# One level of Strassen's algorithm for the second product of a fused attention and ELU kernel

## The chip, the cores and the metric

The kernel runs on one core of one Trainium2 chip. The metric is device time in microseconds (us). Five engines are named as the profile names them: PE (TensorE matmuls; PEld is its weight loads), DVE (VectorE), ACT (ScalarE), POOL (GpSimd) and SP (SyncE, which issues most DMAs).

## The reference

```python
# x: (8, 8, 512, 64) float32, state: (8, 8, 32, 64) float32      B, H, S, D and 32 states
scores = x @ state.T / 8;   a  = softmax(scores);   xread = a @ state     # per batch and head
scores2 = state @ x.T / 8;  a2 = softmax(scores2);  sread = a2 @ x
t = concat([xread, sread], axis=2)         # (8, 8, 544, 64), as a matrix (8*544, 512)
h = t @ w_in                               # w_in (512, 2048)
g = where(h > 0, h, exp(min(h, 0)) - 1)    # ELU
out = g @ w_out                            # w_out (2048, 512)
```

Output: 4352 rows of 512 float32. The weights arrive as float64, and the kernel makes float32 of them.

## The kernel before, in words

Each of the 8 batches has 512 tokens. For a batch the kernel computes both softmaxes (`attention`), folds `state` into `w_in` (`make_m`, tile `m_sb`), and then runs two products. The **first product** (`ffn1`) makes 16 tiles h of 128 hidden features by 512 tokens, with two matmuls each, in a PSUM pool of three banks. ACT and DVE make the ELU of each tile (`exp_part`: two ACT passes into `e_sb`; `max_part`: one DVE pass into `g_sb`). The **second product** (`ffn2_part`) takes the 16 tiles of `g_sb` as weights in four chunks of 128 tokens; each chunk accumulates 16 matmuls of 512 columns of `w_out` in one PSUM bank, and `ffn2_end` copies the bank to `o_sb`. The 8*32 state rows go last (`states`): a first product with 256 columns and two chunks of the second product.

Batch 0 (`first_batch`) follows a plan written out by hand, beside which ACT and DVE convert the weights; its second product runs all four chunks together. From batch 1 on, PE and SP keep the order in which the program is written, while a scheduler orders ACT, DVE and POOL. Inside the second product of batch b the steps of the attention of batch b+1 are hung in as hooks, one after every four matmuls of the code: two steps of transposes of x (`xT_ps`), the scores (`s_ps`, followed by the softmax on DVE, ACT and POOL), two empty ones, the transposes of the state softmax (`sT_ps`), the state read (`sr_ps`), the load of x for batch b+2; `full_m` (`m_ps`) is hung in at chunk 3. They share one PSUM slot of two banks, `ps_a`. Batch 7 has no hooks.

A matmul of the code in float32 is two MATMUL records in the trace, each with its own LDWEIGHTS, so a batch's second product is 4*16*2 = 128 records. Nearly all instructions are recorded through one helper, and so have one line, L93; they are told apart by their tiles.

Of the kernel before, what the change touches and what calls it, by code (L numbers as in the profile page):

```python
# [10 lines left out]
FP32 = mybir.dt.float32  # L11
# [4 lines left out]
ALU = mybir.AluOpType  # L16
# [9 lines left out]
def kernel(  # L26
# [31 lines left out]
    out_b = out.rearrange("(b s) c -> b s c", b=B)  # L58
# [4 lines left out]
    def pool(name, bufs, **kw):  # L63
        return ctx.enter_context(tc.tile_pool(name=name, bufs=bufs, **kw))

    cpool = pool("const", 1)
    xpool = pool("x", 2)
    apool = pool("attn", 2)
    atspool = pool("aT_s", 1)
    xtpool = pool("xT", 2)  # L70
    atpool = pool("aT", 4)
    mpool = pool("m", 2)
    rawpool = pool("raw", NRAW)
    small = pool("small", 4)
    gpool = pool("g", FO + 1)
    epool = pool("elu", 4)
    opool = pool("o", 2)
    ps_a = pool("ps_a", 1, space=PSUM)
    ps_h = pool("ps_h", 3, space=PSUM)
# [30 lines left out]
    w_in = cpool.tile([P, NP, DF], FP32, name="w_in")  # L110
    w_out = cpool.tile([P, FO, DM], FP32, name="w_out")

    kT = cpool.tile([P, B, P], FP32, name="kT")

    xT_state = cpool.tile([P, NP, B * NS], FP32, name="xT_state")
# [9 lines left out]
            )  # L125

    def load_states():
        raw = rawpool.tile([P, B, G, D], FP32, tag="raw", name="s_sb")
        s_v = state.rearrange("b (m c) n d -> m c n b d", c=G)
        for m in range(NP):  # L130
            for c in range(G):
                sync.dma_start(out=raw[m * NS : (m + 1) * NS, :, c], in_=s_v[m, c])
        return raw
# [5 lines left out]

    def load_weights(src):  # L140
        k = src.shape[-1]
        raw = rawpool.tile([P, 512], moe_w_in.dtype, tag="raw", name="raw")
        sync.dma_start(out=raw.rearrange("p (j k) -> p j k", k=k), in_=src)
        return raw

# [54 lines left out]
        st[b, "xT", i] = ps  # L200

    def copy_x(b, i):
        xT = xtpool.tile([P, 2, R * P], FP32, name="xT")
        for j in range(2):
            st[b, 2 * i + j] = xT[:, j]
            scalar.copy(
                out=xT[:, j], in_=st[b, "xT", i][:, j].rearrange("p r q -> p (r q)")
            )
# [84 lines left out]
                transpose(ps[:, g, r], a[:, r])  # L293

    def copy_state(b):
        st[b, "aT_s"] = atspool.tile([P, G, R, P], FP32, name="aT_s")
        for g in range(G):
            scalar.copy(out=st[b, "aT_s"][:, g], in_=st[b, "sT"][:, g])

# [30 lines left out]
    def full_m(b, c):  # L330
        make_m(b, c)
        copy_m(b, c, (scalar.copy, vector.tensor_copy))

    def elu(ps, g, fo):

        e = exp_part(ps)
        max_part(g, fo, e, ps)

    def exp_part(ps):
        e = epool.tile([P, ps.shape[-1]], FP32, tag="e", name="e_sb")  # L340
        scalar.activation(out=e, in_=ps, func=AF.Relu, scale=-1.0)
        scalar.activation(out=e, in_=e, func=AF.Exp, scale=-1.0)
        return e

    def max_part(g, fo, e, ps):
        g[fo] = gpool.tile([P, ps.shape[-1]], FP32, tag="g", name="g_sb")
        vector.scalar_tensor_tensor(
            out=g[fo], in0=e, scalar=-1.0, in1=ps, op0=ALU.add, op1=ALU.max
        )

    def ffn1(g, b, fo):

        ps = ps_h.tile([P, S], FP32, tag="h", name="h_ps")
        for k in range(G):
            matmul(
                ps,
                m_t[b, fo // 4][:, k, fo % 4 * P : (fo % 4 + 1) * P],
                st[b, k, "aT"],
                start=(k == 0),
                stop=(k == G - 1),  # L360
            )
        return ps

    def ffn1_state(g, fo):

# [9 lines left out]
        elu(ps, g, fo)

    def ffn2_part(g, chunks, ps, fos, hooks=(), every=1):

        done = 0
        for fo in fos:  # L380
            for c in chunks:
                matmul(
                    ps[c],
                    g[fo][:, c * P : (c + 1) * P],
                    w_out[:, fo],
                    start=(fo == 0),
                    stop=(fo == FO - 1),
                )
                done += 1
                if hooks and done % every == 0:  # L390
                    hooks.pop(0)()

    def o_bank():
        return ps_o.tile([P, DM], FP32, tag="o", name="o_ps")

    def ffn2_end(chunks, ps, o_sb):
        for c in chunks:
            (scalar.copy, vector.tensor_copy)[c % 2](out=o_sb[c // 2][:, c % 2], in_=ps[c])

    def attention(b):  # L400

# [19 lines left out]

    def store(b, i, o_sb):
        rows = out_b[b, 0:S].rearrange("(p r) c -> p r c", r=R)
        sync.dma_start(out=rows[:, 2 * i : 2 * i + 2], in_=o_sb[i])

    def two_o():
        return [opool.tile([P, 2, DM], FP32, name="o_sb") for i in range(2)]

    def first_batch():

# [24 lines left out]
        for c in range(1, FC + 1):  # L455
            if c < FC:
                order += [lambda c=c, n=n: load_w_in(c, n) for n in range(NP)]
            order += [lambda fo=fo: load_w_out(fo) for fo in range(4 * c - 4, 4 * c)]
        w, h, e, g = [], {}, {}, {}

        def fetch():
            if len(w) == 28:
# [18 lines left out]
        for step in plan:  # L481
            name, _, num = step.partition(":")
            num = [int(i) for i in num.split(".") if i]
            if name == "kT":
                turn_states(raw_states)
            elif name == "kTc":
                vector.tensor_copy(out=kT, in_=st["k_ps"])
                fetch()
            elif name in groups:
                groups[name](*num)  # L490
            elif name in whole:
                whole[name](*num)
            elif name == "w":
                (convert_1, convert_2)[num[1] - 1](*w[num[0]])
                if num[1] == 2:
                    fetch()
            elif name == "F":
                h[num[0]] = ffn1(g, 0, num[0])
            elif name == "R":
                e[num[0]] = exp_part(h[num[0]])  # L500
            elif name == "E":
                max_part(g, num[0], e[num[0]], h[num[0]])
            elif name == "O":
                ffn2_part(g, range(R), o_ps, num)
            elif name == "x":
                turn_x(*num)
            elif name == "M":
                make_m(*num)
            elif name == "xc":
                copy_x(*num)  # L510
            else:
                assert name == "Mc", step
                copy_m(*num, (scalar.copy, scalar.copy))
        copy_m(1, 0, (scalar.copy, vector.tensor_copy))
        o_sb = two_o()
        ffn2_end(range(R), o_ps, o_sb)
        for i in range(2):
            store(0, i, o_sb)

    def batch(b):  # L520
        g = {}
        for fo in range(FO):
            elu(ffn1(g, b, fo), g, fo)
# [6 lines left out]
        o_sb = two_o()  # L530
        for c in range(R):
            if nxt and c == R - 1:
                hooks += [lambda: full_m(b + 1, 0)]
            ps = {c: o_bank()}
            ffn2_part(g, [c], ps, range(FO), hooks, 4)
            ffn2_end([c], ps, o_sb)
            if c % 2:
                store(b, c // 2, o_sb)
        for f in hooks:
            f()  # L540

    def states():
        g = {}
        for fo in range(FO):
            ffn1_state(g, fo)
        o_sb = [opool.tile([P, 2, DM], FP32, name="o_sb")]
        for c in range(2):
            ps = {c: o_bank()}
            ffn2_part(g, [c], ps, range(FO))
            ffn2_end([c], ps, o_sb)  # L550
            for i in range(P // NS):
                sync.dma_start(
                    out=out_b[c * (P // NS) + i, S:SB], in_=o_sb[0][i * NS : (i + 1) * NS, c]
                )
# [38 lines left out]
```

## Time and profile before

| | |
|---|---|
| median of 3 runs | 862.76 us (862.56 to 862.92) |
| the profiled execution's own time | 862.39 us |
| its span | 860.6 us |
| PE busy | 823.3 us, 96% |
| DVE, ACT, POOL busy | 275.8, 303.1, 35.5 us (32%, 35%, 4%) |
| mean granted TensorE clock | 0.994 of 2.4 GHz |

The span is the recorded part of the execution; 1.8 us lie around it. Busy shares say how much an engine does, and the chain of waits says on which engine the end hung.

### The profile page before, as it was taken

To read this page: it belongs to the slowest core of one execution; us is meant where nothing else is said; L and a number is where in the kernel's file an instruction comes from. 1 tells how busy PE (TensorE), PEld (TensorE's weight loads), DVE (VectorE), ACT (ScalarE), POOL (GpSimd) and SP (SyncE) were. 2 spreads that over 40 slices of the span, in tenths; PEclk is the share of its full clock that TensorE was granted. 3 is DMA by queue.
4 is the path that set the end of the run, shared out by engine and by line. 5 is a ranking of instruction groups with operands and counts; after the bars stand their busy time and mean duration, and the time that the engine had idled before them with its cause. 6 is when DMAs were issued, how large, how long until landed. Compare 5 with 4: busy or idle time off the path is not lost.

```text
span 860.6 us, 7230 instructions
## 1 busy us (share of the span) xinstructions
PE 823.3 (96%) x2824; PEld 385.0 (45%) x2824; DVE 275.8 (32%) x510; ACT 303.1 (35%) x534; POOL 35.5 (4%) x38
## 2 busy tenths in 40 slices
PE   2299999999999999999999999999999999999997
PEld 2044455345444454345434543445434544444763
DVE  1999944423033401432032402440042303300110
ACT  2889833631045202630064103620163104500320
POOL 0200001001000200010000200020000200000000
PEclk9889999999999999999999999999999999999999
DMA  9356400500030003000030003000000000000000
GB/s 236 129 196 201 141 0 38 111 1 15 10 73 1 2 24 74 0 1 25 0 74 0 1 25 73 1 0 25 24 1 1 14 11 24 1 0 25 24 1 24
DMA packets 42786, 35.07 MB, mean 41 GB/s; under 512 B 36352, under 2 KB 36352, under 8 KB 42752
## 3 DMA queue, kind: packets, MB, share of 16 engines
q1 hardware_dynamic: 38592, 33.56, 13.7%
q10 hardware_dynamic: 4160, 1.05, 0.7%
q8 instruction: 22, 0.36, 0.2%
q14 instruction: 12, 0.10, 0.0%
HBM read 25.69 MB, written 8.91 MB: 40 GB/s over the span
## 4 chain that ended last, share of the span: by engine, by line
PE 91%; DVE 6%; DMA 2%; ACT 0%; issue 0%; ACTq 0%; SPq 0%
PE o_ps L93 53%; PE h_ps L93 28%; PE m_ps L93 3%; PE sr_ps L93 3%; DVE w_in L93 3%; PE xT_ps L93 2%; DVE w_out L93 2%; PE s_ps L93 1%; DMA x_sb<-in_x_dram 1%; PE sT_ps L93 1%; DMA raw<-in_moe_w_in_dram 0%; DVE g_sb L93 0%; DMA s_sb<-in_state_dram 0%; DVE total_t L93 0%; ACT xT L93 0%
## 5 line engine op out<-in xcount | busy, mean ns | idle before, releaser
L93 PE MATMUL o_ps<-w_out,g_sb 128*128 128x512 f32 x1088 | 478.9, 594 | 0.3 <-DVE w_out L93 0.3
L93 PEld LDWEIGHTS o_ps<-w_out,g_sb 128*128 128x128 f32 x1088 | 203.3, 190 | 252.9 <-issue 247.9
L93 PE MATMUL h_ps<-aT,m_sb 128*128 128x512 f32 x512 | 231.7, 603 | 9.0 <-DVE aT L93 8.0
L93 PEld LDWEIGHTS h_ps<-aT,m_sb 128*128 128x128 f32 x512 | 96.0, 192 | 141.2 <-issue 115.1
L93 DVE SCALAR_TENSOR_TENSOR g_sb<-e_sb,h_ps 128x512 f32<-128x512 f32 (+1 forms) x144 | 94.6, 658 | 166.3 <-ACT e_sb L93 166.3
L93 ACT ACTIVATE e_sb<-h_ps 128x512 f32<-128x512 f32 (+1 forms) x144 | 82.6, 574 | 170.1 <-PE h_ps L93 169.8
L93 ACT ACTIVATE e_sb<-e_sb 128x512 f32<-128x512 f32 (+1 forms) x144 | 87.5, 608 | 4.6
L93 ACT COPY o_sb<-o_ps 128x512 f32<-128x512 f32 x17 | 9.8, 581 | 190.9 <-PE o_ps L93 190.9
L93 DVE COPY o_sb<-o_ps 128x512 f32<-128x512 f32 x17 | 11.7, 691 | 150.5 <-PE o_ps L93 150.5
L93 DVE COPY m_sb<-m_ps 128x512 f32<-128x512 f32 x28 | 19.2, 686 | 113.7 <-ACT m_sb L93 113.7
L93 PE MATMUL m_ps<-w_in,kT 64*32 64x512 f32 x512 | 37.5, 615 | 6.9 <-ACT a_s L93 6.8
L93 ACT ACTIVATE raw<-raw 128x512 f32<-128x512 uint32 x64 | 43.6, 681 | 1.0
L93 POOL TENSOR_TENSOR t_sb<-t_sb,top_t 128x512 f32<-128x512 f32 x16 | 17.1, 1074 | 621.4 <-DVE top_t L93 608.7
L93 ACT COPY xT<-xT_ps 128x512 f32<-128x512 f32 x32 | 17.2, 588 | 53.0 <-PE xT_ps L93 53.0
L93 DVE TENSOR_REDUCE top<-s_ps 128x1 f32<-128x512 f32 x16 | 11.1, 692 | 71.0 <-PE s_ps L93 69.7
L93 ACT COPY m_sb<-m_ps 128x512 f32<-128x512 f32 x36 | 20.3, 576 | 34.1 <-PE m_ps L93 34.1
L93 PEld LDWEIGHTS sr_ps<-aT_s,x_sb 128*128 128x128 f32 x256 | 29.8, 192 | 3.8 <-issue 3.6
L93 PE MATMUL sr_ps<-aT_s,x_sb 128*128 128x64 f32 x256 | 29.4, 273 | 0.0
L93 PE MATMUL h_ps<-xT_state,w_in 128*128 128x256 f32 x128 | 27.8, 379 | 0.0
L93 PEld LDWEIGHTS h_ps<-xT_state,w_in 128*128 128x128 f32 x128 | 24.3, 190 | 3.7 <-issue 0.5
L93 ACT ACTIVATE a_s<-s_ps,top 128x512 f32<-128x512 f32 x16 | 11.0, 689 | 34.7 <-DVE top L93 29.4
L93 PEld LDWEIGHTS m_ps<-w_in,kT 64*32 64x32 f32 x512 | 6.0, 105 | 33.9 <-issue 23.5
(39 smaller groups left out, 279.9 us busy)
## 6 DMA issues: line engine op xcount, KB each, us to landing
raw<-in_moe_w_in_dram SPq DMA_DIRECT2D x16, 512.0 KB, 4.9
raw<-in_moe_w_out_dram SPq DMA_DIRECT2D x16, 512.0 KB, 4.3
out_dram<-o_sb SPq DMA_DIRECT2D x16, 512.0 KB, 2.7
x_sb<-in_x_dram SPq DMA_DIRECT2D x28, 256.0 KB, 5.0
x_sb<-in_x_dram ACTq DMA_DIRECT2D x4, 256.0 KB, 6.8
s_sb<-in_state_dram SPq DMA_DIRECT2D x8, 64.0 KB, 5.1
out_dram<-o_sb SPq DMA_DIRECT2D x8, 64.0 KB, 1.7
```

What stands on the lines that cost most here:

```text
L93: ins = getattr(self.engine, name)(*args, **kw)
```

## The change

The matrix product of one half batch (256 tokens by 2048 features, times `w_out`) is split once into 2 by 2 blocks: tokens in two groups of 128, features in even and odd tiles (`e`), output columns in two halves of 256. Seven block products take the place of eight, in Winograd's form: four sums of blocks of g and four of `w_out`, and the products accumulated in two PSUM banks `a` and `b`, with copies and adds into `o_sb` in between. Batches 1 to 7 have two halves each, the states one; batch 0 keeps its second product. The sums of `w_out` are made once, after batch 0, on DVE: `t_w[1]` = b12 - b11, `t_w[2]` = b22 - `t_w[1]`, `t_w[4]` = b21 - `t_w[2]`, and `t_w[3]` = b22 - b12, which overwrites b12. In the class, `copy` takes 256 columns of a bank to a part of `o_sb` on ACT, and `add` adds 256 columns of a bank to a part of `o_sb` on DVE; a bank goes on accumulating after it was copied.

```diff
-    atspool = pool("aT_s", 1)
-    xtpool = pool("xT", 2)
-    rawpool = pool("raw", NRAW)
-    gpool = pool("g", FO + 1)
-    epool = pool("elu", 4)
+    work = pool("work", NRAW + 4)
+    epool = pool("elu", 3)
...
+    g_all = cpool.tile([P, FO, S], FP32, name="g_all")
...
-    def max_part(g, fo, e, ps):
-        g[fo] = gpool.tile([P, ps.shape[-1]], FP32, tag="g", name="g_sb")
+    def max_part(fo, e, ps):
         vector.scalar_tensor_tensor(
-            out=g[fo], in0=e, scalar=-1.0, in1=ps, op0=ALU.add, op1=ALU.max
+            out=g_all[:, fo, : ps.shape[-1]], in0=e, scalar=-1.0, in1=ps,
+            op0=ALU.add, op1=ALU.max,
         )
...
+    w_k = w_out.rearrange("p (k e) (h q) -> p k e h q", e=2, h=2)
+    b11, b12, b21, b22 = (w_k[:, :, e, h] for e in range(2) for h in range(2))
+    def weight_sum(i):
...
+            vector.tensor_tensor(out=t_w[i][j], in0=x, in1=y, op=ALU.subtract)
+    class Strassen:
...
+        def sums(self):
...
+            for out, x, y, op in (
+                (self.s1, self.a21, self.a22, ALU.add),
+                (self.s2, self.s1, self.a11, ALU.subtract),
+                (self.a21, self.a11, self.a21, ALU.subtract),
+            ):
+                vector.tensor_tensor(out=out, in0=x, in1=y, op=op)
+        def product(self, ps, a, b, first=False, last=False):
+            for k in range(FO // 2):
+                matmul(
+                    ps[:, : DM // 2], a[:, k], b(k),
+                    start=first and k == 0, stop=last and k == FO // 2 - 1,
+                    skip_group_check=True,
+                )
...
+            def p1():
+                ps["a"] = o_bank()
+                self.product(ps["a"], self.a11, lambda k: b11[:, k], first=True)
+                self.copy(ps["a"], 0, 0)
+            def p2():
+                ps["b"] = o_bank()
+                self.product(ps["b"], self.a12, lambda k: b21[:, k], first=True, last=True)
+                self.add(ps["b"], 0, 0)
+                vector.tensor_tensor(
+                    out=self.a12, in0=self.a12, in1=self.s2, op=ALU.subtract
+                )
+            def p6():
+                self.product(ps["a"], self.s2, t(2))
+                self.copy(ps["a"], 1, 0)
+            def p7():
+                ps["b"] = o_bank()
+                self.product(ps["b"], self.a21, t(3), first=True)
+                self.copy(ps["b"], 1, 1)
+            def p5():
+                self.product(ps["a"], self.s1, t(1))
+                self.add(ps["a"], 1, 1)
+            def p4():
+                self.product(ps["b"], self.a22, t(4), last=True)
+                self.add(ps["b"], 1, 0)
+            def p3():
+                self.product(ps["a"], self.a12, lambda k: b22[:, k], last=True)
+                self.copy(ps["a"], 0, 1)
+            return [p1, p2, p6, p7, p5, p4, p3]
...
     def batch(b):
...
-        for c in range(R):
-            if nxt and c == R - 1:
-                hooks += [lambda: full_m(b + 1, 0)]
-            ps = {c: o_bank()}
-            ffn2_part(g, [c], ps, range(FO), hooks, 4)
-            ffn2_end([c], ps, o_sb)
+        two = [Strassen(i) for i in range(2)]
+        two[0].sums()
+        for i in range(2):
+            for n, f in enumerate(two[i].steps()):
+                f()
+                if (i, n) == (0, 3):
+                    two[1].sums()
+                if (i, n) == (1, 3) and nxt:
+                    hooks += [lambda: full_m(b + 1, 0)]
+                if hooks:
+                    hooks.pop(0)()
+            store(b, i, two[i].o_sb)
     def states():
...
+        half = Strassen(0)
+        half.sums()
+        for f in half.steps():
             f()
+        for b in range(B):
+            c, i = divmod(b, P // NS)
+            sync.dma_start(out=out_b[b, S:SB], in_=half.o_sb[i * NS : (i + 1) * NS, c])
+    for i in (1, 2, 4, 3):
+        weight_sum(i)
```

On PE, in the second product of batch 1, the program before has the four chunks, with hooks between pieces of four matmuls:

```order
L93 MATMUL h_ps<-aT,m_sb 128x512 x12
L93 MATMUL o_ps<-w_out,g_sb 128x512 x4
L93 MATMUL xT_ps<-ident,x_sb 128x128 x8
L93 MATMUL o_ps<-w_out,g_sb 128x512 x4
L93 MATMUL xT_ps<-ident,x_sb 128x128 x8
L93 MATMUL o_ps<-w_out,g_sb 128x512 x4
L93 MATMUL s_ps<-xT,kT 32x512 x8
L93 MATMUL o_ps<-w_out,g_sb 128x512 x12
L93 MATMUL sT_ps<-ident,a_s 128x128 x8
L93 MATMUL o_ps<-w_out,g_sb 128x512 x4
```

The changed program at the same place has p1, p2, p6, p7, p5, p4 and p3 of the first half, 8 matmuls each; `s_1052` and `s_1051` are the sums s2 and s1 of this half:

```order
L92 MATMUL h_ps<-aT,m_sb 128x512 x12
L92 MATMUL o_ps<-w_out,g_all 128x256 x8
L92 MATMUL xT_ps<-ident,x_sb 128x128 x8
L92 MATMUL o_ps<-w_out,g_all 128x256 x8
L92 MATMUL xT_ps<-ident,x_sb 128x128 x8
L92 MATMUL o_ps<-t_w,s_1052 128x256 x8
L92 MATMUL s_ps<-xT,kT 32x512 x8
L92 MATMUL o_ps<-w_out,g_all 128x256 x8
L92 MATMUL o_ps<-t_w,s_1051 128x256 x8
L92 MATMUL o_ps<-t_w,g_all 128x256 x8
L92 MATMUL sT_ps<-ident,a_s 128x128 x8
L92 MATMUL o_ps<-w_out,g_all 128x256 x8
```

Each hook stands behind one block product of 8 matmuls of half the width, where it stood behind four matmuls.

On DVE the same second product now begins with sums (`s_1169` and `s_1170` are s1 and s2 of the second half), which stand ahead of the softmax of the next batch:

```order
L92 SCALAR_TENSOR_TENSOR g_all<-e_sb,h_ps 128x512 x6
L92 TENSOR_TENSOR s_1051<-g_all 128x1024
L92 TENSOR_TENSOR s_1052<-s_1051,g_all 128x1024
L92 TENSOR_TENSOR g_all<-g_all 128x8x128
L92 TENSOR_TENSOR o_sb<-o_sb,o_ps 128x256
L92 TENSOR_TENSOR g_all<-g_all,s_1052 128x8x128
L92 TENSOR_TENSOR s_1169<-g_all 128x1024
L92 TENSOR_TENSOR g_all<-g_all 128x8x128
L92 TENSOR_TENSOR s_1170<-s_1169,g_all 128x1024
L92 TENSOR_REDUCE top<-s_ps 128x1
L92 STREAM_TRANSPOSE t_sb<-s_ps 128x512
```

Before, the row of six maxima was followed at once by the reduction of `s_ps`. `s_1170` takes the buffer of `s_1052`, so it waits for the end of p6; the reduction stands behind it. Further on, the add of p5 stands behind most of that softmax:

```order
L92 TENSOR_SCALAR a_s<-a_s,total 128x512 x2
L92 TENSOR_REDUCE total_t<-t_sb 128x16
L92 STREAM_TRANSPOSE aT<-t_sb 128x512
L92 TENSOR_SCALAR total_t<-total_t 128x16
L92 TENSOR_TENSOR o_sb<-o_sb,o_ps 128x256
L92 RECIPROCAL total_t<-total_t 128x16
```

On DVE at the passage from batch 0 to batch 1 the eight weight sums stand between the transposes of `aT` and the copy of `m_sb`:

```order
L92 STREAM_TRANSPOSE aT<-t_sb 128x512
L92 TENSOR_TENSOR t_w<-w_out 128x1024
L92 STREAM_TRANSPOSE aT<-t_sb 128x512
L92 TENSOR_TENSOR t_w<-w_out 128x1024
L92 TENSOR_TENSOR t_w<-w_out,t_w 128x1024 x3
L92 COPY xT_state<-sr_ps 64x4x32 x2
L92 TENSOR_TENSOR t_w<-w_out,t_w 128x1024
L92 TENSOR_TENSOR w_out<-w_out 128x4x256 x2
L92 COPY m_sb<-m_ps 128x512
```

Before, only the two `xT_state` copies stood there.

## Rows read from the trace of the kernel before

**Rows 1.** The page: chain that ended last, shares by engine.
```profile
PE 91%; DVE 6%; DMA 2%; ACT 0%; issue 0%; ACTq 0%; SPq 0%
```

**Rows 2.** Timeline of PE, batch 7 into states: start, length, instructions, count.
```profile
745.78 55.10 PE L93 MATMUL o_ps<-w_out,g_sb 128*128 128x512 f32 x128
800.71 27.79 PE L93 MATMUL h_ps<-xT_state,w_in 128*128 128x256 f32 x128
828.34 27.63 PE L93 MATMUL o_ps<-w_out,g_sb 128*128 128x512 f32 x64
```

**Rows 3.** Timeline of PEld in the states' first product.
```profile
800.71 27.39 PEld L93 LDWEIGHTS h_ps<-xT_state,w_in 128*128 128x128 f32 x127 [0.24 <-issue]
```

**Rows 4.** Groups by form: busy us, mean ns of one, idle before.
```profile
L93 PEld LDWEIGHTS h_ps<-xT_state,w_in 128*128 128x128 f32 x128 | 24.3, 190 | 3.7 <-issue 0.5
```

**Rows 5.** Timeline of PE, second product of batch 2.
```profile
272.36 3.60 PE L93 MATMUL o_ps<-w_out,g_sb 128*128 128x512 f32 x8
275.79 1.04 PE L93 MATMUL xT_ps<-ident,x_sb 128*128 128x128 f32 x8
276.67 3.60 PE L93 MATMUL o_ps<-w_out,g_sb 128*128 128x512 f32 x8
284.50 1.09 PE L93 MATMUL s_ps<-xT,kT 64*32 64x512 f32 x16
285.52 10.57 PE L93 MATMUL o_ps<-w_out,g_sb 128*128 128x512 f32 x24
295.93 1.04 PE L93 MATMUL sT_ps<-ident,a_s 128*128 128x128 f32 x8
296.80 3.60 PE L93 MATMUL o_ps<-w_out,g_sb 128*128 128x512 f32 x8
```

**Rows 6.** Groups by form: sizes near those of the sums, adds and copies.
```profile
L93 DVE COPY kT<-k_ps 128x1024 f32<-128x1024 f32 x1 | 1.2, 1224 | 2.8 <-PE k_ps L93 2.8
L93 DVE SCALAR_TENSOR_TENSOR g_sb<-e_sb,h_ps 128x256 f32<-128x256 f32 x16 | 6.7, 421 | 21.5 <-ACT e_sb L93 21.5
L93 POOL TENSOR_TENSOR t_sb<-t_sb,total_t 128x512 f32<-128x512 f32 x16 | 17.9, 1117 | 17.9 <-DVE total_t L93 17.9
L93 DVE TENSOR_SCALAR w_out<-w_out 128x512 f32<-128x512 f32 x16 | 6.7, 418 | 0.0
L93 ACT ACTIVATE e_sb<-h_ps 128x256 f32<-128x256 f32 x16 | 6.1, 384 | 28.3 <-PE h_ps L93 28.3
```

**Rows 7.** Timeline of DVE, second product of batch 2.
```profile
273.85 0.69 DVE L93 SCALAR_TENSOR_TENSOR g_sb<-e_sb,h_ps 128x512 f32<-128x512 f32 x1 [1.03 <-ACT e_sb L93]
285.70 0.69 DVE L93 TENSOR_REDUCE top<-s_ps 128x1 f32<-128x512 f32 x1 [11.16 <-PE s_ps L93]
291.33 2.24 DVE L93 TENSOR_SCALAR a_s<-a_s,total 128x512 f32<-128x512 f32 x2
294.71 0.13 DVE L93 TENSOR_SCALAR total_t<-total_t 128x16 f32<-128x16 f32 x1
```

**Rows 8.** Timeline of ACT, the same place.
```profile
289.50 0.57 ACT L93 COPY o_sb<-o_ps 128x512 f32<-128x512 f32 x1
```

**Rows 9.** Timelines of DVE, POOL and PE, passage from batch 0 to batch 1.
```profile
134.54 0.66 DVE L93 STREAM_TRANSPOSE aT<-t_sb 128x512 f32<-128x512 f32 x1
134.77 1.05 POOL L93 TENSOR_TENSOR t_sb<-t_sb,total_t 128x512 f32<-128x512 f32 x1 [0.46 <-DVE total_t L93]
135.85 0.71 DVE L93 STREAM_TRANSPOSE aT<-t_sb 128x512 f32<-128x512 f32 x1 [0.66 <-POOL t_sb L93]
141.24 0.59 DVE L93 COPY xT_state<-sr_ps 64x128 f32<-64x128 f32 x2 [4.68 <-PE sr_ps L93]
146.43 0.69 DVE L93 COPY m_sb<-m_ps 128x512 f32<-128x512 f32 x1 [4.61 <-ACT m_sb L93]
```

**Rows 10.** Timeline from the last matmul on: DVE, and the issues of SP.
```profile
856.01 0.69 DVE L93 COPY o_sb<-o_ps 128x512 f32<-128x512 f32 x1 [26.18 <-PE o_ps L93]
856.73 1.73 SPq L93 DMA_DIRECT2D out_dram<-o_sb  x4
```

More of the change, by code (lines that the diff above doesn't have):

```diff
@@ L127, in load_states @@
     def load_states():
-        raw = rawpool.tile([P, B, G, D], FP32, tag="raw", name="s_sb")
+        raw = work.tile([P, B, G, D], FP32, tag="w", name="s_sb")
         s_v = state.rearrange("b (m c) n d -> m c n b d", c=G)
@@ L141, in load_weights @@
         k = src.shape[-1]
-        raw = rawpool.tile([P, 512], moe_w_in.dtype, tag="raw", name="raw")
+        raw = work.tile([P, 512], moe_w_in.dtype, tag="w", name="raw")
         sync.dma_start(out=raw.rearrange("p (j k) -> p j k", k=k), in_=src)
@@ L202, in copy_x @@
     def copy_x(b, i):
-        xT = xtpool.tile([P, 2, R * P], FP32, name="xT")
+        xT = work.tile([P, 2, R * P], FP32, tag="w", name="xT")
         for j in range(2):
@@ L295, in copy_state @@
     def copy_state(b):
-        st[b, "aT_s"] = atspool.tile([P, G, R, P], FP32, name="aT_s")
+        st[b, "aT_s"] = work.tile([P, G, R, P], FP32, tag="w", name="aT_s")
         for g in range(G):
@@ L332, in full_m @@
         copy_m(b, c, (scalar.copy, vector.tensor_copy))
-    def elu(ps, g, fo):
-        e = exp_part(ps)
-        max_part(g, fo, e, ps)
     def exp_part(ps):
@@ L343, in exp_part, with elu, ffn1 @@
         return e
-    def max_part(g, fo, e, ps):
-        g[fo] = gpool.tile([P, ps.shape[-1]], FP32, tag="g", name="g_sb")
+    def max_part(fo, e, ps):
         vector.scalar_tensor_tensor(
-            out=g[fo], in0=e, scalar=-1.0, in1=ps, op0=ALU.add, op1=ALU.max
-        )
-    def ffn1(g, b, fo):
+            out=g_all[:, fo, : ps.shape[-1]], in0=e, scalar=-1.0, in1=ps,
+            op0=ALU.add, op1=ALU.max,
+        )
+    def elu(ps, fo):
+        max_part(fo, exp_part(ps), ps)
+    def ffn1(b, fo):
         ps = ps_h.tile([P, S], FP32, tag="h", name="h_ps")
@@ L362, in ffn1, with ffn1_state @@
         return ps
-    def ffn1_state(g, fo):
+    def ffn1_state(fo):
         ps = ps_h.tile([P, B * NS], FP32, tag="h", name="h_ps")
@@ L374, in ffn1_state @@
             )
[L375 to L391, printed above, removed]
+        elu(ps, fo)
@@ L393, in o_bank, with ffn2_row @@
+    def ffn2_row(ps, fo):
+        for c in range(R):
+            matmul(
+                ps[c],
+                g_all[:, fo, c * P : (c + 1) * P],
+                w_out[:, fo],
+                start=(fo == 0),
+                stop=(fo == FO - 1),
+            )
     def o_bank():
         return ps_o.tile([P, DM], FP32, tag="o", name="o_ps")
-    def ffn2_end(chunks, ps, o_sb):
-        for c in chunks:
-            (scalar.copy, vector.tensor_copy)[c % 2](out=o_sb[c // 2][:, c % 2], in_=ps[c])
+    w_k = w_out.rearrange("p (k e) (h q) -> p k e h q", e=2, h=2)
@@ new lines @@
+    b11, b12, b21, b22 = (w_k[:, :, e, h] for e in range(2) for h in range(2))
+    t_w = {}
+    def weight_sum(i):
+        halves = [slice(k, k + FO // 4) for k in (0, FO // 4)]
+        if i == 3:
+            t_w[3] = [b12[:, k] for k in halves]
+        else:
+            t_w[i] = [work.tile([P, FO // 4, DM // 2], FP32, tag="w", name="t_w") for k in halves]
+        for j, k in enumerate(halves):
+            x, y = {
+                1: lambda: (b12[:, k], b11[:, k]),
+                2: lambda: (b22[:, k], t_w[1][j]),
+                3: lambda: (b22[:, k], b12[:, k]),
+                4: lambda: (b21[:, k], t_w[2][j]),
+            }[i]()
+            vector.tensor_tensor(out=t_w[i][j], in0=x, in1=y, op=ALU.subtract)
@@ new lines, with __init__, part, copy @@
+    class Strassen:
+        def __init__(self, s):
+            a = g_all.rearrange("p (k e) (s h q) -> p k e s h q", e=2, h=2, q=P)
+            (self.a11, self.a21), (self.a12, self.a22) = (
+                [a[:, :, e, s, h] for h in range(2)] for e in range(2)
+            )
+            self.o_sb = opool.tile([P, 2, DM], FP32, name="o_sb")
+        def sums(self):
+            self.s1, self.s2 = (
+                work.tile([P, FO // 2, P], FP32, tag="w", name=n) for n in ("s1", "s2")
+            )
+            for out, x, y, op in (
[6 more added lines that the diff above has]
+            for k in range(FO // 2):
+                matmul(
+                    ps[:, : DM // 2], a[:, k], b(k),
+                    start=first and k == 0, stop=last and k == FO // 2 - 1,
+                    skip_group_check=True,
+                )
+        def part(self, h, q):
+            return self.o_sb[:, h, q * DM // 2 : (q + 1) * DM // 2]
+        def copy(self, ps, h, q):
+            scalar.copy(out=self.part(h, q), in_=ps[:, : DM // 2])
+        def add(self, ps, h, q):
+            vector.tensor_tensor(
+                out=self.part(h, q), in0=self.part(h, q), in1=ps[:, : DM // 2], op=ALU.add
+            )
+        def steps(self):
+            t = lambda i: lambda k: t_w[i][k // (FO // 4)][:, k % (FO // 4)]
+            ps = self.ps = {}
+            def p1():
[6 more added lines that the diff above has]
+                self.add(ps["b"], 0, 0)
+                vector.tensor_tensor(
+                    out=self.a12, in0=self.a12, in1=self.s2, op=ALU.subtract
+                )
+            def p6():
[15 more added lines that the diff above has]
+            return [p1, p2, p6, p7, p5, p4, p3]
@@ L423, in store @@
         rows = out_b[b, 0:S].rearrange("(p r) c -> p r c", r=R)
-        sync.dma_start(out=rows[:, 2 * i : 2 * i + 2], in_=o_sb[i])
-    def two_o():
-        return [opool.tile([P, 2, DM], FP32, name="o_sb") for i in range(2)]
+        sync.dma_start(out=rows[:, 2 * i : 2 * i + 2], in_=o_sb)
     def first_batch():
@@ L458, in first_batch @@
             order += [lambda fo=fo: load_w_out(fo) for fo in range(4 * c - 4, 4 * c)]
-        w, h, e, g = [], {}, {}, {}
+        w, h, e = [], {}, {}
         def fetch():
@@ L497, in first_batch @@
             elif name == "F":
-                h[num[0]] = ffn1(g, 0, num[0])
+                h[num[0]] = ffn1(0, num[0])
             elif name == "R":
@@ L501, in first_batch @@
             elif name == "E":
-                max_part(g, num[0], e[num[0]], h[num[0]])
+                max_part(num[0], e[num[0]], h[num[0]])
             elif name == "O":
-                ffn2_part(g, range(R), o_ps, num)
+                ffn2_row(o_ps, num[0])
             elif name == "x":
@@ L514, in first_batch @@
         copy_m(1, 0, (scalar.copy, vector.tensor_copy))
-        o_sb = two_o()
-        ffn2_end(range(R), o_ps, o_sb)
         for i in range(2):
+            o_sb = opool.tile([P, 2, DM], FP32, name="o_sb")
+            for c in range(2):
+                (scalar.copy, vector.tensor_copy)[c](out=o_sb[:, c], in_=o_ps[2 * i + c])
             store(0, i, o_sb)
     def batch(b):
-        g = {}
         for fo in range(FO):
-            elu(ffn1(g, b, fo), g, fo)
+            elu(ffn1(b, fo), fo)
             if fo % 4 == 1 and fo // 4 + 1 < FC:
@@ L529, in batch, with states @@
             hooks += [lambda: load_x(b + 2, [sync])]
-        o_sb = two_o()
-        for c in range(R):
-            if nxt and c == R - 1:
-                hooks += [lambda: full_m(b + 1, 0)]
-            ps = {c: o_bank()}
-            ffn2_part(g, [c], ps, range(FO), hooks, 4)
-            ffn2_end([c], ps, o_sb)
-            if c % 2:
-                store(b, c // 2, o_sb)
-        for f in hooks:
-            f()
[L542 to L554, printed above, removed]
+        two = [Strassen(i) for i in range(2)]
[10 more added lines that the diff above has]
+            store(b, i, two[i].o_sb)
+    def states():
+        for fo in range(FO):
+            ffn1_state(fo)
+        half = Strassen(0)
+        half.sums()
+        for f in half.steps():
+            f()
+        for b in range(B):
+            c, i = divmod(b, P // NS)
+            sync.dma_start(out=out_b[b, S:SB], in_=half.o_sb[i * NS : (i + 1) * NS, c])
     first_batch()
```

## The prediction

> **What bounds the kernel now.** I began with the chain that ended last [rows 1]: 91% of the span hangs on PE. So only PE time, or something that makes PE wait, moves the end. Then I read PE's timeline of the last batch, which has no hooks [rows 2]. The second product starts at 745.78 and the states' first product at 800.71: 54.93 us for 128 records of 512 columns, 0.4291 us each, with no gap. The states' first product, of 256 columns, starts at 800.71 and is followed at 828.34: 27.63 us for 128 records, 0.2159 us each. So a record costs what its columns cost, and halving them halves it. Third, the weight loads of that stretch [rows 3, 4]: 127 loads merge into one piece of 27.39 us, each 190 ns long. They fit under matmuls of 216 ns, with 26 ns to spare. Last, DVE around a second product [rows 7]: it is idle for 11.16 us before the softmax of the next batch, and there the new sums must go.
>
> **What the change removes on PE.** A batch had 4 chunks of 16 matmuls, two records each: 128 records, 54.93 us. Now it has 2 halves of 7 products of 8 matmuls: 224 records of 256 columns. By 0.2159 us these take 48.35 us, 6.58 us less; over seven batches 46.1 us. The states had 64 records (27.46 us) and get 112 (24.18 us): 3.3 us less. Together 49.3 us, if no product waits. The hooks on PE are the same in number and size.
>
> One rule of the Trainium skill speaks against this, and rows 2 to 4 show the opposite first: there each 128-row load of 190 ns lies wholly beside a 256-column matmul. The rule ("TensorE: Matmul & The Clock Gate", Part 3, The mechanism) is that a weight load overlaps running matmuls only if it is for another group of rows, and all loads here are for the whole array; by it, a record would be load plus matmul, which is the slower rival below. The trace disagrees with the rule.
>
> **What it adds on DVE, and whether PE waits for it.** The trace has no DVE addition of two float32 tiles in SBUF. The nearest rows [rows 6]: a DVE copy of the same 1024 elements took 1.224 us; a POOL tensor_tensor of 512 took 1.117, which is 2.23 for 1024; a DVE tensor_scalar of 512 took 0.418, which is 0.84. I take 1.22, the same engine and size, and keep 0.84 and 2.23 as ends. For an add of 256 columns I take 0.42, the two-input DVE pass of that size; for an ACT copy of 256 columns 0.38.
>
> Now one half with its hooks, from T = 0 where the second product starts (272.36 in batch 2 [rows 5]). A product is 16 * 0.2159 = 3.45 us, the transposes of a hook 0.88 (275.79 to 276.67), the scores 1.02 (284.50 to 285.52), the state's transposes 0.87 (295.93 to 296.80).
> - The last tile of g was ready at 274.54, T+2.18 [rows 7]. Then s1 and s2 follow, to T+4.62. PE does p1, a hook, p2, a hook, and reaches p6 at T+8.66: 4.0 us to spare. In batch 7, without hooks, p6 comes at T+6.90, and 2.3 us are left.
> - p2 ends at T+7.78. DVE then adds it (0.42) and makes three sums, to T+11.86. s2 of the second half waits for p6, which ends at T+12.11, and is done at T+13.33. Queued behind it is the softmax. Its first reduction came 1.20 us after the start of the scores (284.50 to 285.70 [rows 5, 7]), which is T+13.31: practically no delay.
> - From that reduction on I keep the distances of the trace. ACT's free copy lies 3.80 us later [rows 8]; p7's copy there ends by T+17.5, and p4, which needs its bank, starts at T+20.03. `a_s` is scaled after 7.87 us, T+21.2 [rows 7]; PE wants it at T+23.48, after p4. The add of p5 stands behind the small pass that ended at 294.84: 9.14 + 0.42 us, T+22.9. p3 needs that bank at T+24.35.
>
> The smallest margin is 1.46 us, so I cost the sums at nothing. If the cover goes, PE pays what exceeds it, in the six second products that have hooks. In the second half no softmax stands on DVE, and margins are larger. The first product has as much DVE work as before.
>
> **The passage to batch 1.** Eight sums of `w_out` come after the first transposes of `aT`, which end at 135.20 [rows 9]: 8 * 1.22, plus 0.71 and 0.59 for the passes between them, ends at 146.3. The copy of `m_sb`, for which PE waits, stands behind them and came at 146.43. The `xT_state` copies, which free the PSUM slot for `m_ps`, end at 142.6 instead of 141.8; the slot is needed some 1.6 us (1.02 for such a piece on PE, 0.57 on ACT [rows 5, 8]) before 146.43. So nothing, but only just. At 2.23 us per sum it would cost 8.0 us; at 0.84 it gains nothing, since PE holds the time.
>
> A POOL pass runs here from 134.77 to 135.82 [rows 9], and the two scalings of `a_s` beside POOL took 2.24 us [rows 7] against 0.42 for another such pass [rows 6]. The Trainium skill ("SBUF — State Buffer", SBUF: two separate sides) has it that a DVE pass with two SBUF inputs and a POOL pass shut each other out for a whole instruction; the slow pair agrees. By that rule the first sum starts 0.62 us later, and the estimate would rise by 0.5 us. I leave it out of the sum.
>
> **The end.** Before, the last chunk was copied in 0.69 us and four stores issued in 1.73 us, 0.43 each [rows 10]; the first four were issued earlier. Now p3 fills columns of the first 128 rows, SP sends those rows first, and so all eight stores queue behind p3's copy: 1.73 us more, less 0.31 for the narrower copy: +1.4 us. Ends: nothing, if the stores overlap better; 3.5 us, if all eight are new.
>
> **Smaller parts.** The shared pool has eleven buffers where weights had seven, so loads may start earlier in batch 0; the second product of batch 0 keeps its work. Three `e_sb` buffers instead of four go with three h banks, which are held longer. I take nothing for each; no row here bounds it, and the low end of the range leaves 2 us for it.
>
> **Sum.** 862.39 (the profiled execution) - 49.3 + 1.4 = 814.5 us. The median of runs is 0.37 us above that execution, so 814.8.
>
> **Rivals.**
> - *DVE becomes late.* If a sum costs 2.23 us, the three sums behind p2 end at T+14.9, s2 at T+17.1, and the softmax starts 3.8 us late; less 1.46 that is 2.3 us of waiting at p3, six times 14 us, plus 8.0 at the passage: 837. It decides from 1.65 us per sum on. For it: the margin is thin and no row has the operation. Against: all DVE passes of 512 or 1024 elements from PSUM run at one speed, and DVE does not slow down from SBUF in rows 6.
> - *Each product starts cold.* If each of the 105 products (14 in each of seven batches, 7 in the states) had to show its first weight load, since it waits for a copy or a sum, that is 105 * 0.19 = 20 us: 835. Against: the 0.2159 us of rows 2 hold the starts of 16 accumulations, each waiting for a bank, and pieces of `o_ps` behind hooks take 3.60 us as others do [rows 5].
> - *Weight loads come out from under the matmul (slower).* The 1680 records before cost 411.97 us in their old form, so with the tail the change breaks even at 0.244 us a record, 29 ns above the row. With load and matmul one after the other, 0.406 us: 682 us, and 1134 in all. For it: loads become 1.75 times as many in the second product and have 26 ns of room. Against: rows 3 show no gap in 127.
>
> **How the numbers follow.** My forecast has 0.80, with its own range of 813 to 818; late DVE 0.08, cold starts 0.08, bare weight loads 0.03, and 0.01 for a change that nothing above makes and that leaves the time within 0.2%, about what a measurement of this kernel can tell. The range reaches from 812.8 (no added tail, and a little less in batch 0) to 822, which takes in the milder forms of the first two rivals. All but the last two cases are faster: 0.96; same 0.01; slower 0.03.
>
> **What will show it.** Second product of batch 7: 224 records in 48.4 us without a gap. In batches 1 to 6, PE's waits for `o_sb`, sums or copies near zero. DVE sums of 1024 near 1.22 us, and the reduction of `s_ps` some 1.2 us after the scores start. The copy of `m_sb` at the passage ending about when it did. Eight stores after the last copy. I am wrong if the records of 256 columns take over 0.22 us, or if p3 or p6 stands waiting for DVE in each batch.

## The result and the profile after

| | before | changed |
|---|---|---|
| median | 862.77 us (862.56 to 862.92, 4 runs) | 815.13 us (815.01 to 815.28, 4 runs) |
| profiled execution, its span | 862.39, 860.6 us | 815.28, 813.5 us |
| PE, PEld busy | 823.3, 385.0 us | 773.9, 521.8 us |
| DVE, ACT busy | 275.8, 303.1 us | 362.1, 316.3 us |

The ratio is 0.9448 (95% interval 0.9432 to 0.9464): faster by 47.6 us, 0.3 us from the forecast.

The end still hangs on PE. This is the page's chain by engine, which answers to [rows 1]:

```profile
PE 91%; DVE 6%; DMA 1%; ACT 1%; issue 0%; ACTq 0%
```

The timeline of PE from the second product of batch 7 on answers to [rows 2] (start, length, instructions, count):

```profile
706.98 7.07 PE L92 MATMUL o_ps<-w_out,g_all 128*128 128x256 f32 x32
713.89 3.62 PE L92 MATMUL o_ps<-t_w,s 128*128 128x256 f32 x16
717.34 3.62 PE L92 MATMUL o_ps<-w_out,g_all 128*128 128x256 f32 x16
...
755.33 27.79 PE L92 MATMUL h_ps<-xT_state,w_in 128*128 128x256 f32 x128
782.96 7.07 PE L92 MATMUL o_ps<-w_out,g_all 128*128 128x256 f32 x32
...
803.68 3.62 PE L92 MATMUL o_ps<-w_out,g_all 128*128 128x256 f32 x16
```

A product of 16 records starts every 3.45 us (713.89 to 717.34), whether it reads sums or not. The second product lasts from 706.98 to 755.33, 48.35 us where [rows 2] had 54.93. From the start of batch 1's first product to the end of the last record it is 660.1 us (147.18 to 807.30) instead of 709.5 (146.45 to 855.97): 49.4 us saved.

Who PE waited for (us in total, times, longest), all waits of the changed kernel:

```profile
PE k_ps L92 <- DMA s_sb<-in_state_dram: 13.6, 1, 13.6
PE h_ps L92 <- DVE aT L92: 8.0, 1, 8.0
PE m_ps L92 <- ACT a_s L92: 6.9, 1, 6.9
PE xT_ps L92 <- DVE kT L92: 1.3, 1, 1.3
PE xT_ps L92 <- ACT xT L92: 1.2, 1, 1.2
PE s_ps L92 <- ACT xT L92: 1.2, 1, 1.2
PE h_ps L92 <- ACT m_sb L92: 0.7, 1, 0.7
PE o_ps L92 <- DVE w_out L92: 0.3, 1, 0.3
PE h_ps L92 <- DVE g_all L92: 0.2, 1, 0.2
```

None of them is a sum, an add or a copy of Strassen's; the list of before has the same nine entries (there the tile of g is `g_sb`), with 12.9 us in the first and the others within 0.1 us. The new work has the sizes that were taken from [rows 6] (groups by form: busy us, mean ns of one, idle before):

```profile
L92 DVE TENSOR_TENSOR s<-s,g_all 128x1024 f32<-128x1024 f32 x15 | 18.4, 1225 | 2.2 <-PE o_ps L92 1.9
L92 DVE TENSOR_TENSOR o_sb<-o_sb,o_ps 128x256 f32<-128x256 f32 x45 | 18.6, 414 | 128.9 <-PE o_ps L92 75.0 <-issue 53.8
L92 ACT COPY o_sb<-o_ps 128x256 f32<-128x256 f32 x60 | 22.2, 371 | 265.1 <-PE o_ps L92 265.1
```

DVE in the second product of batch 2 (its timeline; PE begins that second product at 266.50) answers to [rows 7]:

```profile
269.97 1.23 DVE L92 TENSOR_TENSOR s<-s,g_all 128x1024 f32<-128x1024 f32 x1
...
277.26 1.23 DVE L92 TENSOR_TENSOR g_all<-g_all 128x1024 f32<-128x1024 f32 x1
278.81 1.23 DVE L92 TENSOR_TENSOR s<-s,g_all 128x1024 f32<-128x1024 f32 x1 [0.32 <-PE o_ps L92]
279.95 0.68 DVE L92 TENSOR_REDUCE top<-s_ps 128x1 f32<-128x512 f32 x1
...
288.99 0.40 DVE L92 TENSOR_TENSOR o_sb<-o_sb,o_ps 128x256 f32<-128x256 f32 x1
```

The sums before the last one were done 0.32 us before p6 ended, and the add of p5 ended at 289.39, 22.89 us after the second product began. PE's timeline has p3, which needs the bank of that add:

```profile
291.06 3.62 PE L92 MATMUL o_ps<-w_out,g_all 128*128 128x256 f32 x16
```

So the margin is 1.67 us. In batch 1 p3 starts after the same 24.56 us (178.40 to 202.96).

At the passage to batch 1 (timeline of DVE; answers to [rows 9]):

```profile
135.84 1.78 DVE L92 TENSOR_TENSOR t_w<-w_out 128x1024 f32<-128x1024 f32 x1
...
138.17 1.18 DVE L92 TENSOR_TENSOR t_w<-w_out 128x1024 f32<-128x1024 f32 x1
...
144.43 2.35 DVE L92 TENSOR_TENSOR w_out<-w_out 128x1024 f32<-128x1024 f32 x2
147.16 0.69 DVE L92 COPY m_sb<-m_ps 128x512 f32<-128x512 f32 x1 [0.37 <-ACT m_sb L92]
```

The weight sums end at 146.78, and DVE then waits 0.37 us for ACT before it copies `m_sb`: they were hidden, by 0.37 us. The first took 1.78 us and the second 1.18; a POOL pass ran from 135.49 to 136.54.

The end answers to [rows 10] (timelines of ACT and SP):

```profile
807.33 0.37 ACT L92 COPY o_sb<-o_ps 128x256 f32<-128x256 f32 x1 [9.99 <-PE o_ps L92]
807.73 3.64 SPq L92 DMA_DIRECT2D out_dram<-o_sb  x8
```

Eight issues follow the last copy, and the span ends 2.1 us after the last of them (811.37 to 813.5), as before (858.46 to 860.6). From the last record to the end of the span it is 6.2 us, before 4.6.

### The profile page after: what moved, and what is told of

Same layout as the page of the kernel before. It is cut to its first block, busy times and chain, and to the rows that moved or that the text cites. A ratio compares the mean times of both kernels' runs of the same rounds, so it can differ in the third digit from the quotient of the medians.

```text
span 813.5 us, 8814 instructions
## 1 busy us (share of the span) xinstructions
PE 773.9 (95%) x3544; PEld 521.8 (64%) x3544; DVE 362.1 (45%) x608; ACT 316.3 (39%) x579; POOL 35.5 (4%) x38
## 4 chain that ended last, share of the span: by engine, by line
PE 91%; DVE 6%; DMA 1%; ACT 1%; issue 0%; ACTq 0%
PE o_ps L92 50%; PE h_ps L92 30%; PE m_ps L92 4%; PE sr_ps L92 3%; DVE w_in L92 3%; PE xT_ps L92 2%; DVE w_out L92 2%; PE s_ps L92 1%; DMA x_sb<-in_x_dram 1%; PE sT_ps L92 1%; DVE g_all L92 0%; DMA s_sb<-in_state_dram 0%; DVE total_t L92 0%; ACT xT L92 0%; PE k_ps L92 0%
## 5 line engine op out<-in xcount | busy, mean ns | idle before, releaser
L92 PE MATMUL o_ps<-w_out,g_all 128*128 128x256 f32 (+1 forms) x1088 | 274.4, 405 | 0.3 <-DVE w_out L92 0.3
L92 PEld LDWEIGHTS o_ps<-w_out,g_all 128*128 128x128 f32 x1088 | 204.2, 190 | 62.5 <-issue 35.8
L92 DVE SCALAR_TENSOR_TENSOR g_all<-e_sb,h_ps 128x512 f32<-128x512 f32 (+1 forms) x144 | 94.6, 658 | 192.3 <-ACT e_sb L92 192.3
L92 ACT COPY o_sb<-o_ps 128x256 f32<-128x256 f32 (+1 forms) x62 | 23.3, 378 | 265.1 <-PE o_ps L92 265.1
L92 PE MATMUL o_ps<-t_w,s 128*128 128x256 f32 x480 | 109.1, 380 | 0.0
L92 PEld LDWEIGHTS o_ps<-t_w,s 128*128 128x128 f32 x480 | 90.2, 190 | 16.8 <-ACT o_sb L92 5.0
L92 DVE TENSOR_TENSOR o_sb<-o_sb,o_ps 128x256 f32<-128x256 f32 x45 | 18.6, 414 | 128.9 <-PE o_ps L92 75.0
L92 PE MATMUL o_ps<-t_w,g_all 128*128 128x256 f32 x240 | 54.2, 379 | 0.0
L92 PEld LDWEIGHTS o_ps<-t_w,g_all 128*128 128x128 f32 x240 | 45.6, 190 | 6.2
```

The costliest lines, as they stand in the source:

```text
L92: ins = getattr(self.engine, name)(*args, **kw)
```

## The experiments

Times are medians. Each experiment ran in rounds beside the kernel before on one chip, on three chips in all, and the medians of the kernel before there were 862.73 to 862.87 us. "The change" is 815.13 us.

**1. The layout alone.** The changed kernel with the second product of before:

```diff
-        two = [Strassen(i) for i in range(2)]
...
+            for fo in range(FO):
+                matmul(
+                    ps, g_all[:, fo, c * P : (c + 1) * P], w_out[:, fo],
+                    start=(fo == 0), stop=(fo == FO - 1),
+                )
...
-    for i in (1, 2, 4, 3):
-        weight_sum(i)
```

> Only the other parts of the change: one tile for all of g, the shared pool, three e buffers. The second product is done in chunks of 512 columns as before, and there are no sums. Theory (the time is PE's records by their columns): no gain, 862.8 us, or 863.5 if the 0.7 us by which batch 0 starts later in the changed kernel comes from the shared pool. Rival (the pools or the joint tile bring part of the gain): clearly below 862 us.

Measured: 862.54 us, ratio 0.9998 (0.9989 to 1.0007). Pools and layout bring nothing and cost nothing that the interval, about 1 us either way, can tell.

**2. Narrow matmuls without Strassen.** The kernel before, with this in batches 1 to 7:

```diff
+        for q in range(2):
+            cols = slice(q * 256, (q + 1) * 256)
+            for fo in range(FO):
+                matmul(
+                    ps[:, cols], g[fo][:, c * P : (c + 1) * P], w_out[:, fo, cols],
+                    start=(fo == 0), stop=(fo == FO - 1),
+                )
```

> The kernel before, but in batches 1 to 7 each second product matmul of 512 columns is two of 256, so twice the weight loads and no Strassen. Theory (a load of 190 ns lies beside a matmul of 216 ns): 256 records * 0.2159 - 54.93 = 0.33 us more a batch, 865.1 us in all. Rival (loads come out from under narrow matmuls): at 0.406 us a record 49 us more a batch, about 1206 us; already 0.01 us more a record would show as 18 us.

Measured: 864.93 us, ratio 1.0026 (1.0016 to 1.0036), 2.2 us more. PE's timeline of batch 7:

```profile
747.69 55.42 PE L93 MATMUL o_ps<-w_out,g_sb 128*128 128x256 f32 x256
802.95 27.79 PE L93 MATMUL h_ps<-xT_state,w_in 128*128 128x256 f32 x128
```

256 records take 55.26 us, 0.2159 each, with twice the weight loads of 54.93 us. The gain of the change in a batch is the 32 fewer of 256 times that, 6.91 us, less the 0.33 us that the narrow form costs: 6.58 us.

**3. The states as before.**

```diff
-        half = Strassen(0)
-        half.sums()
-        for f in half.steps():
-            f()
+        for c in range(2):
+            ps = o_bank()
+            for fo in range(FO):
+                matmul(
+                    ps, g_all[:, fo, c * P : (c + 1) * P], w_out[:, fo],
+                    start=(fo == 0), stop=(fo == FO - 1),
+                )
```

> The changed kernel with the states' second product in two chunks of 512 columns as before, its stores as before. The 256 columns that hold b12 have been overwritten by then, so the state rows come out other than the reference's. Theory: 3.3 us more for PE, 1.6 us less at the end, where only four stores follow the last copy: 816.8 us. Rival (the saving comes only where hooks lie between products): 813.5 us.

Measured: 816.49 us, ratio 0.9465 (0.9452 to 0.9478), 1.4 us more than the change. The intervals of the two ratios overlap, but the runs do not (816.39 to 816.74 against 815.01 to 815.28), and the trace shows both terms of the expected 1.7:

```profile
782.48 27.63 PE L92 MATMUL o_ps<-w_out,g_all 128*128 128x512 f32 x64
```

The states' second product takes 27.63 us, where the change takes 24.34 (782.96 to 807.30): 3.3 us more. From the last record to the end it is 4.6 us instead of 6.2.

**4. The order of the last stores.**

```diff
-        for b in range(B):
+        for b in (4, 5, 6, 7, 0, 1, 2, 3):
```

> The changed kernel, but the last eight stores go out with rows 128 to 255 first, whose parts are complete after p4. Theory (all eight queue behind p3's copy, 0.43 us each): four issues move under p3, 1.7 us less, 813.4 us. Rival (the end hangs on the landing of the data, not on the issues): no change, 815.1 us.

Measured: 812.87 us, ratio 0.9422 (0.9410 to 0.9435), 2.3 us less than the change, of which 1.7 were expected. The profiled execution, 813.40, the slowest of five, lies 1.9 us below the change's, and SP's timeline has all of that:

```profile
804.34 5.13 SPq L92 DMA_DIRECT2D out_dram<-o_sb  x8
```

The last issue ends at 809.47 instead of 811.37, and the span again 2.1 us after it (811.6). So with eight stores of 64 KB the issues hold the end.

**5. One DVE pass more ahead of the softmax.**

```diff
-                (self.s1, self.a21, self.a22, ALU.add),
+                *[(self.s1, self.a21, self.a22, ALU.add)] * (1 + extra),
...
-                    two[1].sums()
+                    two[1].sums(1 if nxt else 0)
```

> The changed kernel with one more DVE pass of 1024 elements (s1 of the second half, made twice) ahead of the softmax in batches 1 to 6. In the changed kernel's trace the sums ended 0.3 us before p6 did and the add of p5 1.6 us before p3 wanted its bank. Theory (margin): 0.9 us later, still inside the margin, no change, 815.1 us. Rival (each pass on DVE costs PE something): up to 6 * 1.2 = 7 us more, 822 us.

Measured: 814.95 us, ratio 0.9446 (0.9433 to 0.9458). Six passes of 1.22 us cost nothing: DVE's work is not paid while it stays inside the margin. In batch 1 the add of p5 ends at 202.04 and p3 starts at 202.85, so 0.81 us were left.

**6 and 7. Three and six passes more at the head of a second product.** The same edit of `sums`, with `two[0].sums(3)` and `two[0].sums(6)`.

> The changed kernel with s1 of the first half made four times instead of once, in batches 1 to 7 (three passes more, 1.2 us each, ahead of s2). Theory: s2 is ready 8.4 us after the second product starts, p6 comes at 8.7, so batches 1 to 6 lose nothing (the softmax starts 1.5 us late, inside its margin); batch 7 has no hooks, p6 comes at 6.9, 1.5 us lost: 816.6 us. Rival (DVE passes are paid each time): 7 * 3.6 = 25 us more, 840 us.

Measured: 816.95 us, ratio 0.9469 (0.9456 to 0.9482), 1.8 us more than the change. Its waits of PE have one new entry, for p6 of batch 7:

```profile
PE o_ps L92 <- DVE s L92: 1.6, 1, 1.6
```

In batch 1 the add of p5 ends at 201.92 and p3 starts at 202.50: 0.58 us were left.

> The same with s1 made seven times (six passes more). Theory: s2 is ready about 12.5 us after the start, p6 waits some 3.7 us in batches 1 to 6 and 5.5 us in batch 7: 28 us more, 843 us. Rival (no cover at all): 7 * 7.3 = 51 us more, 866 us; rival (all hidden): 815 us.

Measured: 857.73 us, ratio 0.9939 (0.9926 to 0.9953), 42.6 us more. The wait is as forecast, the time is not. Waits of PE for the sums, and PE's timeline at p6 of batch 1:

```profile
PE o_ps L92 <- DVE s L92: 27.7, 7, 5.5
```

```profile
190.77 5.41 PE L92 MATMUL o_ps<-t_w,s 128*128 128x256 f32 x16 [3.70 <-DVE s L92]
```

After 3.70 us of waiting, p6 takes 5.41 us instead of 3.62. The stretches around it (busy time and records of PE, PEld, DVE, ACT and POOL, then the granted clock, the DMA share and GB/s):

```profile
187.00:190.70 3.70, 0.07 (x1) 0.00 (x0) 3.63 (x5) 1.07 (x2) 0.00 (x0) 1.00 0.00 0
190.70:192.50 1.80, 1.73 (x5) 1.45 (x6) 1.80 (x3) 0.00 (x0) 0.00 (x0) 0.65 0.04 9
192.50:194.50 2.00, 2.00 (x6) 1.56 (x6) 1.97 (x3) 0.00 (x0) 0.00 (x0) 0.50 0.00 0
```

Here the granted clock is full while PE waits, and falls to 0.50, the lower of its two levels (1.2 GHz), when it works again. In batches 2, 3, 5 and 6 it had begun to fall within the wait (mean over it 0.78 to 0.94). But not each such wait is followed by a low clock. In batch 4 p6 ran at 1.00 behind the same wait:

```profile
472.92 3.72 PE L92 MATMUL o_ps<-t_w,s 128*128 128x256 f32 x16 [3.70 <-DVE s L92]
```

Behind the six waits of 3.70 us p6 took 5.41, 6.53, 5.19, 3.72, 6.25 and 6.73 us, and behind the 5.54 us of batch 7 it took 5.23. That is 13.7 us above seven times 3.62, and with the 27.7 us of waiting it makes 41.4 of the 42.6 us. In experiment 6 the wait of 1.6 us left the clock at 1.00 (p6 took 3.69 us). That suggested the next test.

**8. The same wait, with PE busy in it.** Experiment 7 (`head6` in the expectation) with

```diff
+            self.first = s == 0 and not over
...
             def p6():
+                if self.first:
+                    idle = ps_h.tile([P, S], FP32, tag="h", name="idle")
+                    self.product(idle, self.a11, lambda k: b11[:, k], first=True, last=True)
                 self.product(ps["a"], self.s2, t(2))
```

> As head6 (s1 of the first half made seven times, batches 1 to 7), but PE does another product of 16 records, read by nobody, ahead of the first half's p6, 3.45 us of the 3.7 to 5.5 us for which it waited. In head6 PE waited 27.7 us for the sums, yet the time rose by 42.6 us, and behind each wait p6's 16 records took 5.2 to 5.4 us instead of 3.62, at a granted clock of 0.50 in the middle. Theory (the rest is the clock that falls while PE waits): p6 starts when it did, at full clock; 27.7 us and some 2 us are left, about 844 to 845 us. Rival (the seven passes disturb something else, such as DVE's later work): 857 us again.

Measured: 846.04 us, ratio 0.9803 (0.9790 to 0.9817), 11.7 us less than experiment 7, though PE does seven products more. PE's timeline and one of the same stretches:

```profile
186.84 3.62 PE L92 MATMUL idle<-w_out,g_all 128*128 128x256 f32 x16
190.71 3.72 PE L92 MATMUL o_ps<-t_w,s 128*128 128x256 f32 x16 [0.24 <-DVE s L92]
```

```profile
192.50:194.50 2.00, 2.00 (x17) 1.49 (x24) 1.97 (x3) 0.04 (x1) 0.00 (x0) 1.00 0.00 0
```

p6 starts at the same time, at full clock, in its usual time. So the second part of experiment 7's loss was the clock, and the rival falls. The expectation puts p6 of experiment 7 at 5.2 to 5.4 us behind each wait; that holds for three of the seven. In batch 7 the product did not fill the wait, and behind the 2.08 us that were left the clock was at 0.50 again:

```profile
743.15 5.38 PE L92 MATMUL o_ps<-t_w,s 128*128 128x256 f32 x16 [2.08 <-DVE s L92]
```

Six delays of 3.87 us (186.84 to 190.71), 5.70 in batch 7 (737.45 to 743.15) and the 1.76 us by which p6 is slow there make 30.7 of the 30.9 us that remain.

**9. Two stores for the states instead of eight.**

```diff
-        for b in range(B):
-            c, i = divmod(b, P // NS)
-            sync.dma_start(out=out_b[b, S:SB], in_=half.o_sb[i * NS : (i + 1) * NS, c])
+        for c in (1, 0):
+            sync.dma_start(
+                out=out_b[c * (P // NS) : (c + 1) * (P // NS), S:SB], in_=half.o_sb[:, c]
+            )
```

> The changed kernel with two stores for the states instead of eight, 256 KB each, rows 128 to 255 first. Theory: one issue of 0.43 us after p3's copy instead of eight, and a landing some 0.5 us longer for the larger transfer: 2.6 us less, 812.5 us. Rival (the end hangs on the landing): 815 us or more.

Measured: 816.08 us, ratio 0.9458 (0.9446 to 0.9471), 1.0 us more than the change, where 2.6 less were expected. SP has its two issues behind it earlier, but the end comes later:

```profile
804.19 3.94 SPq L92 DMA_DIRECT2D out_dram<-o_sb  x2
```

From the end of the last issue to the end of the span it is 6.2 us (808.13 to 814.3), where the change and experiment 4 have 2.1. So here the landing holds the end; my theory took it for nearly the same as that of a small store. The busy share of the 16 DMA engines in tenths and the bandwidth over the last 11 us, in 40 slices, here:

```profile
DMA  0000015050022122222232122222222100000000
GB/s 0 0 0 0 0 45 45 0 22 7 7 67 67 60 97 104 104 104 104 97 82 45 22 82 74 82 104 104 104 104 97 60 15 0 0 0 0 0 0 0
```

and with the eight stores of experiment 4, over 9 us:

```profile
DMA  0000000002837373810000002837282810000000
GB/s 0 0 0 0 0 0 0 0 0 73 200 82 200 82 191 82 209 46 0 0 0 0 0 0 73 200 91 191 73 219 55 218 46 0 0 0 0 0 0 0
```

A store of 256 KB in this form does not pass 104 GB/s and keeps the engines busy to two tenths; stores of 64 KB reach 200 GB/s and more, at seven or eight tenths. Size alone is not the reason: in the change a batch's store of 512 KB, also from 128 partitions, reaches 410 GB/s (235 to 241 us, over 6 us in 40 slices):

```profile
GB/s 0 0 0 0 0 0 0 0 0 0 0 0 382 410 410 382 410 410 410 410 273 0 0 0 0 0 0 0 0 0 0 0 0 0 0 0 0 0 0 0
```

The slow form differs in that one store writes to four batches at once. Whether that is the reason was not tried.

**10. Two queues for the last four stores.** Experiment 4 (`stores` in the expectation) and

```diff
+            queue = scalar if b in (1, 3) else sync
+            queue.dma_start(out=out_b[b, S:SB], in_=half.o_sb[i * NS : (i + 1) * NS, c])
```

> As stores (rows 128 to 255 first), and the last four stores shared by two queues, two on SP and two on ACT. Theory (an issue takes 0.43 us on its queue): two issues fewer behind each other, 0.8 us less than stores, 812.0 us. Rival (ACT's issues are slower, or the landing decides): 812.9 us or more.

Measured: 812.33 us, ratio 0.9416 (0.9403 to 0.9429), the fastest, 2.8 us below the change. Against experiment 4 it is 0.5 us less by medians, but the runs overlap (812.07 to 812.78 and 812.68 to 813.40): not settled. In the two traces the last issue ends 1.3 us after the last record instead of 2.2, and the span 3.7 us after it instead of 4.3.

## Why the prediction was right

*Terms on PE.* 224 records in 48.35 us was the forecast and the measurement, and the 49.3 us in all came out as 49.4. Experiment 2 shows the term by itself: loads of 190 ns stay hidden under 216 ns also with `g` as weights, and the rival of bare weight loads falls. The Trainium skill ("TensorE: Matmul & The Clock Gate", Part 3, The mechanism) has it that a weight load overlaps running matmuls only if it is for another group of rows; the 0.2159 us a record of experiment 2 disagree with that. One reading of the prediction was loose: rows 3 do not show loads without a gap, since 127 of 190 ns fill 24.1 of the 27.39 us; it is PE's stretch in rows 2 that has none. Experiment 1 shows that pools and layout contribute nothing that can be measured.

*Cold starts.* No product shows one: in batch 7 and the states starts are 3.45 us apart across changes of bank and operand.

*DVE.* The price of a sum was forecast as 1.22 and is 1.22 us. In the second product of batch 2 the add of p5 ends 22.89 us after the start (forecast 22.9), the margin is 1.67 (forecast 1.46). Experiments 5 to 7 show that PE waits only for what exceeds a margin: one pass more is free, three make PE wait 1.6 us where batch 7 has no hooks, six make it wait 27.7 us, which the distances gave as 28. What was exceeded there is the margin ahead of p6. The smallest one, ahead of p3, was used up to 0.58 us but never exceeded, so what PE pays there rests on the distances. Late DVE was a real rival, only its condition was not met: a sum took 1.22 us, and it needed 1.65.

*Passage.* Hidden, as forecast, with 0.37 us left instead of 0.1. The first sum did run 0.6 us longer beside POOL, in the change and in all eight experiments that make it, and the slack took it. The Trainium skill ("SBUF — State Buffer", SBUF: two separate sides) has it that a DVE pass with two SBUF inputs and a POOL pass that reads SBUF shut each other out for a whole instruction; the 1.78 us agree.

*End.* Forecast 1.4 us, measured 1.6 (6.2 against 4.6 us): eight issues in a row took 3.64 us, 0.455 each, where the forecast had 0.43. Experiment 4 gives it back.

*What was off.* The profiled execution came out at 815.28 instead of 814.5 us. 0.7 us of that lies at the start, where PE waited 13.6 us for the states instead of 12.9. I had taken nothing for it. The kernel of experiment 2, with the old pools, waited 13.2; those with the shared pool waited 13.2 (experiments 1 and 3) to 13.6 us (experiment 4). Whether the shared pool adds a part stays open; by experiment 1 that part cannot be seen in the time. That the median still came within 0.3 us of the forecast is in part luck: before, it lay 0.37 us above the profiled execution, and now it lies 0.15 us below.

*What a late DVE would have cost* may be undersized: the rival counted only PE's waiting, 2.3 us at p3. Experiments 7 and 8 show that p6 behind a wait of 3.70 us took 0.1 to 3.1 us more, by the clock. Waits of 2.3 us at p3 were not tried; the nearest are 1.6 us in experiment 6, behind which the clock stayed at 1.00, and 2.08 us in batch 7 of experiment 8, behind which it was at 0.50.

## What to carry to other kernels

Where PE is busy nearly all the time, price an algebraic saving by records times columns from a stretch of the same width, then look for the first wait: write the second engine's queue down with distances from the trace, and the smallest margin is what the saving hangs on. In experiments 5 to 7 work beside PE was free up to the margin and paid beyond it, and most waits of 3.70 us were paid twice, once as a wait and again in the clock behind it. Ask also what the change does to the last store: here reordering eight DMAs was worth another 2.3 us, and merging them into two cost 1.0.

## What the runs showed of the hardware

- Behind five of six waits of PE of 3.70 us the next product ran in part at a granted clock of 0.50 and took 5.19 to 6.73 us instead of 3.62; behind one it ran at 1.00 in 3.72 us (experiment 7). With 3.45 us of each wait filled by useless records the clock stayed at 1.00 where hardly any wait was left, and the time fell by 11.7 us over seven batches (experiment 8).
- Weight loads of 190 ns for 128 by 128 float32 stayed hidden under matmul records of 256 columns: 256 records took 55.26 us, 0.2159 each (experiment 2).
- A DVE sum of two SBUF tiles took 1.78 us while POOL worked, the next like it 1.18.
- Two stores of 256 KB from 128 partitions to four batches each moved at 104 GB/s at most (experiment 9), eight of 64 KB at up to 219 (experiment 4), one of 512 KB from 128 partitions to one batch at up to 410 (the change).
